# A written order for three chunks instead of two

## The chip, the cores and the metric

The kernel runs on one core of a Trainium2 chip. The metric is the device time of one execution in microseconds (us), as the median of several executions. The five engines are named as in the profile: PE (TensorE: matmuls; its weight loads are shown as PEld), DVE (VectorE), ACT (ScalarE), POOL (GpSimd) and SP (SyncE, which here only issues transfers). Each engine takes its instructions in the order in which they stand in its queue.

## The reference

Four batches of 768 positions go through a windowed attention with 8 heads of 64, and then through a gated feed-forward layer of 1024:

```python
k_sum = k.reshape(B, H, nb, block, D).max(axis=3)      # block 32
v_sum = v.reshape(B, H, nb, block, D).mean(axis=3)
scores_l = where(|i - j| < 16, q @ k.T / 8, -1e9)
scores_s = q @ k_sum.T / 8 + log(32)
a = softmax(concat([scores_l, scores_s]))
x = a @ concat([v, v_sum])                              # B, S, 512 after the heads are joined
h = relu(x @ w_in)                                      # 512 -> 1024
conv = sum over 3 taps of conv_w[k] * h[shifted by k - 1]
out = (h * sigmoid(conv)) @ w_out                       # 1024 -> 512
```

## The kernel before

**Tiles.** The work is cut into 8 chunks of 384 positions (a batch has two). A chunk has four head pairs, so there are 32 attention steps, numbered n = 0 to 31 (chunk n // 4). For each n the keys' windows (`kw`), the block maxima (`ks`), the values (`va`) and block means (`vm`, from the sums `vs` and a matmul `pv`) are prepared; `qk` makes the scores in PSUM, `mx` adds the mask and finds the maxima (DVE), `ex` takes the exponentials with their sums (ACT), `sm` and `rc` make the reciprocals, `nr` normalizes (POOL or DVE); j = 2n + h counts the halves: `tr` j transposes them on PE, `cp` j copies them out (ACT or DVE), `av` n multiplies by the values, `xh` and `xl` split the result into a high and a low part (ACT, DVE).

**The feed-forward part.** A chunk has 8 units u of 128 features. `f` c.u.cc is one quarter of unit u's first product (three matmuls: high by high, low by high, high by low). Then come, in this order, `re` (relu, ACT), `ta` (the middle tap, ACT or DVE), two `cv` (the other taps, DVE), `th` (tanh, ACT), `mu` (the gate, DVE), `gh` and `gl` (high and low part of the gated rows, ACT and POOL). `g` st.fc, called `second` in the code, is a piece of the second product for 128 rows of the output (three matmuls), `ob` copies a finished tile out and stores it. The first product has three PSUM banks: unit u + 3 needs `mu` of unit u. The transposes have one bank, the second product one.

**What sets the order.** Three regimes follow one another:

1. The table `ORDER` is a string of steps. `run` calls them one by one inside `tc.manual_schedule()`, and each engine gets its instructions in just that order. A letter at the end of a step names the engine (a: ACT, p: POOL, v: DVE). `w` 9 is nine idle matmuls on PE.
2. From chunk `FIRST` on, loops write the steps: `unit(c, u, ...)` calls `slot_t` (transposes), `slot_av`, `slot` (preparation of the steps ahead and the scores of n = j // 2), the unit's own steps, and 2 to 4 pieces of the second product. There only PE keeps the order in which the steps are written; a scheduler places the other engines' instructions by its own costs.
3. At the seam, the first `slot` of chunk `FIRST` is held behind the last instructions of the table on SP and DVE (`last`, which `run` fills from the steps that return an instruction: the transfers, and `mu`).

Where a slot's n begins a batch (chunk of even number), the slot also writes `vs`, `pv`, `vm` and `ks` of that n:

```python
            if n < npair:
                if at(n)[3] == 0:
                    vs(n)
                    pv(n)
                    v_mean(n)
                V(n)
                if at(n)[3] == 0:
                    k_max(n)
                kb(n)
```

In chunk c the first unit's slot prepares n = 4c + 6: 14 for chunk 2, 18 for chunk 3. Transfers wait on SP in the order in which they are issued. R loads a pair's keys, K its windows, T and V the values, Q the queries, I and O the weights; M spreads the means.

Of the kernel before, what the change touches and what calls it, by code (L numbers as in the profile page):

```python
# [51 lines left out]
rc1 mx2.0.1 pv1 mx2.0.2 cp1a Q5 mx2.1.0 ex2.0.2 nr1.0p mx2.1.1 ex2.0.1 mx2.1.2 qk3 ex2.1.0 sti1
V2 ex2.1.1 T10 vb0 locw tr2 hii1 ex2.1.2 I3 nr1.1v cp2a win6 mx3.0.0 V3 ex2.0.0 w3 tr3 mx3.0.1
zcw mx3.0.2 av0 wli1 sm2 ex3.0.0 mx3.1.0 mx3.1.1 ex3.1.0 rc2 O0 mx3.1.2 ex3.0.2 qk4 nr2.0v cp3a
stcw ex3.0.1 nr2.1v tr4 I2 vm1 pv2 loi5 ex3.1.2 vb1 cp4v xh0 ex3.1.1 mx4.0.0 xl0 wli0 tr5 sm3
zi5 rc3 av1 mx4.0.1 mx4.0.2 vm2 ex4.0.1 mx4.1.0 sti5 pv3 ex4.0.2 xh1 mx4.1.1 nr3.0p mx4.1.2
ex4.0.0 cp5v qk5 ex4.1.2 kb6 xl1 vb2 hii5 vs10 tr6 ex4.1.0 f0.0.0 nr3.1p cp6a av2 mx5.0.0
# [18 lines left out]
f1.0.3 wlo5 mx9.0.2 hio4 mu0.7 f1.1.2 ex8.0.0 ks10 f1.2.0 re1.0 wlo4 ex8.1.2 f1.1.3 ta1.0v
ex8.0.2 f1.2.1 mx9.1.0 vm10 cv1.0.0 ex8.1.0 M10 gl0.6 g0.4 ex9.1.0 mx9.1.1 K11 cv1.0.2 sm8 re1.1
f1.2.2 M8 kb10 rc8 mx9.1.2 th1.0 nr8.0p pv11 ta1.1v V8 g0.5 zo6 V10 cv1.1.0 nr8.1p tr16 gh0.7
K12 qk10 mu1.0 ex9.1.1 gl0.7 cv1.1.2 ex9.0.0 f1.3.0 ex9.1.2 mx10.0.0 loo6 cp16a f1.2.3 ex9.0.1
sto6 T9 f1.3.1 th1.1 K13 mx10.0.1 tr17 ex9.0.2 mu1.1 f1.3.2 zo7 loo7 f1.4.0 mx10.0.2 hio6  # L80
mx10.1.0 f1.3.3 sto7 sm9 cp17a f1.4.1 vm11 rc9 wlo6 mx10.1.1 ex10.0.0 av8 mx10.1.2 re1.2 ks11
hio7 f1.4.2 nr9.0p ex10.1.1 ta1.2v M12 g0.6 gh1.0 Q12 kb11 cv1.2.0 xh8 wlo7 tr18 ex10.0.2
cv1.2.2 qk11 gh1.1 cp18v ex10.1.0 f1.4.3 nr9.1p th1.2 g0.7 ex10.0.1 gl1.1 mu1.2 tr19 vs9 ob0
f1.5.0 kb12 re1.3 g1.0 mx11.0.0 xl8 ta1.3a f1.5.1 ex10.1.2 cv1.3.0 ex11.0.0 pv9 g1.1 mx11.0.1
sm10 gh1.2 mx11.0.2 rc10 mx11.1.0 f1.5.2 nr10.0p vm9 cv1.3.2 cp19a M9 g1.2 re1.4 mx11.1.1 V9
gl1.2 mx11.1.2 ex11.0.2 f1.5.3 M11 th1.3 Q14 tr20 nr10.1p ex11.1.1 mu1.3 qk12 ex11.1.0 ta1.4v
gl1.0 re1.5 f1.6.0 cv1.4.0 ex11.1.2 g1.3 ex11.0.1 kb13 cv1.4.2 f1.6.1 mx12.0.0 th1.4 av9 cp20a
mu1.4 ta1.5a mx12.0.1 tr21 sm11 cv1.5.0 ex12.0.1 M13 g1.4 xh9 V11 gh1.3 xl9 f1.7.0 V13 cp21a
mx12.0.2 f1.6.2 K15 ex12.0.2 mx12.1.0 cv1.5.2 V12 f1.7.1 ex12.0.0 K14 rc11 th1.5 mx12.1.1 f1.6.3
nr11.0p mx12.1.2 gh1.4 mu1.5 av10 re1.6 gl1.3 ex12.1.0 tr22 xh10 f1.7.2 nr11.1p cp22v ex12.1.2  # L90
qk13 ta1.6v gh1.5 gl1.4 tr23 mx13.0.0 g1.5 gl1.5 mx13.0.1 cv1.6.0 ex13.0.1 f1.7.3 ex12.1.1 xl10
g1.6 cp23a mx13.0.2 cv1.6.2 ex13.0.2 av11 sm12 mx13.1.0 th1.6 rc12 mx13.1.1 nr12.0p mx13.1.2
# [6 lines left out]
def attention_ffn(ctx, tc, qT, kT, vT, k_win, v_nat, v_win, w_in, cwT, w_out, mask8, ident_in, out):  # L99
# [121 lines left out]
    def keys(n):  # L221
        if n not in kw:
            if n == NP - 1:
                t = sp.tile([P, 1024], F32, tag="stage", name=f"kw{n}", bufs=2)
# [46 lines left out]
        nc.vector.tensor_reduce(ks[b, p], kv, AX.X, ALU.max)  # L271

    def win(n):
# [3 lines left out]
        (nc.gpsimd if n else nc.vector).tensor_copy(keys(n)[:, :, :WK], k)  # L277

    def kb(n):
        c, p, b, hf = at(n)  # L280
        nc.gpsimd.tensor_copy(
            keys(n)[:, :, WK:NK], ks[b, p].unsqueeze(1).to_broadcast([P, CB, NB])
        )

# [22 lines left out]
                stop=i == S // P - 1,  # L307
            )

    def v_mean(n):  # L310
# [2 lines left out]
        nc.scalar.activation(vm[b, p], pvs.pop(n)[:NB, :P], AF.Copy, scale=1.0 / BLK)

    def vb(n):
        c, p, b, hf = at(n)
        nc.gpsimd.tensor_copy(
            va[n][WK:NK, :, :], vm[b, p].unsqueeze(1).to_broadcast([NB, CB, P])
        )

# [44 lines left out]
            accum_out=sm[n][:, h, i : i + 1],  # L365
        )

    def sums(n):
        nc.scalar.activation(sm[n], sm[n], AF.Copy, bias=1e-9)

    def rc(n):
        nc.vector.reciprocal(sm[n], sm[n])
# [47 lines left out]
        for new, old in zip(xT[c], xT[c - 1]):  # L420
            nc.vector.tensor_copy(new[:, :, 0:2], old[:, :, CH - 2 : CH].bitcast(F32))  # L421
# [4 lines left out]
    def xl(n):
        h, l = rows(n)
# [21 lines left out]
        hf = c % 2  # L449
        return CH - 1 + 2 * hf, (CH - 1) * hf  # L450

    def re(c, u):
# [1 line left out]
        nc.scalar.activation(h, h, AF.Relu)  # L454
# [46 lines left out]
    def gh(c, u):
        nc.scalar.copy(gate_rows("hi", c, u), conv[c, u])  # L502

    def gl(c, u):
        nc.gpsimd.tensor_tensor(  # L505
            gate_rows("lo", c, u),
            conv.pop((c, u)),
            gate_rows("hi", c, u).bitcast(F32),
            ALU.subtract,
        )  # L510
# [257 lines left out]
```

## Time and profile before

| | us |
|---|---|
| median of 3 runs (390.04 to 390.67) | 390.18 |
| the profiled execution | 390.11 |
| its span | 388.3 |
| PE busy | 370.9 |
| ACT busy | 250.3 |
| DVE busy | 247.0 |
| POOL busy | 150.3 |

The span is the time from the first to the last recorded instruction; what lies around it is 1.8 us in that execution. Busy time is the time in which an engine has at least one instruction under way. PE's matmuls overlap, so a busy PE isn't always at its peak: the granted clock (PEclk) tells at which share of full speed it ran, in tenths in the slices. A row of a timeline gives start, duration, engine, line, operation, output and inputs, and in brackets the idle time ahead and what ended it. A row of the chain of waits gives only start, length and what the time went to. Chunk c starts with its first `f`: chunk 2 at 108.8 us, chunk 3 at 154.6 us, chunk 4 at 195.2 us.

### The profile page before, as it was taken

What the parts mean: (1) busy time and instruction counts of PE and PEld (TensorE: products, weight loads), DVE (VectorE), ACT (ScalarE), POOL (GpSimd) and SP (SyncE); (2) the same over time, 40 slices, a digit from 0 to 9 for tenths busy, and PEclk for the clock granted to TensorE, in tenths of its full rate; (3) what the DMA queues carried; (4) which work ended last, traced back from release to release, by engine and by line L of the source; (5) the groups of instructions that cost most, each with busy time, mean ns of one, the idle gap of its engine ahead of it and who ended that gap; (6) DMA issues with size and microseconds to landing.
All of it is one profiled execution on the core that took longest, in us unless ns stands there. A gap on an engine that the chain in (4) does not pass through costs nothing.

```text
span 388.3 us, 8833 instructions
## 1 busy us (share of the span) xinstructions
PE 370.9 (96%) x3164; PEld 317.8 (82%) x3167; DVE 247.0 (64%) x764; ACT 250.3 (64%) x795; POOL 150.3 (39%) x186
## 2 busy tenths in 40 slices
...
PEclk9999999999969999999989999999999999999999
...
GB/s 281 364 317 329 277 212 284 217 187 122 298 289 245 145 144 132 197 191 88 100 93 103 117 97 101 75 120 95 105 67 0 30 9 20 29 28 27 29 54 54
DMA packets 26859, 55.03 MB, mean 142 GB/s; under 512 B 3072, under 2 KB 11456, under 8 KB 26816
## 3 DMA queue, kind: packets, MB, share of 16 engines
...
q8 instruction: 25, 0.41, 0.5%
...
## 4 chain that ended last, share of the span: by engine, by line
PE 80%; ACT 8%; DVE 6%; DMA 3%; issue 1%; POOL 1%; SPq 0%; ACTq 0%; POOLq 0%; DVEq 0%
PE f L524 31%; PE f L440 30%; PE xp L398 6%; PE pt L384 6%; PE pq L330 5%; ACT a L359 3%; DVE t L474 2%; DMA kT<-kT 2%; DMA kw<-k_win 1%; PE pv L302 1%; ACT t L485 1%; DVE t L492 1%; DVE a L344 1%; ACT wu_i L145 1%; DVE ks L271 1%
## 5 line engine op out<-in xcount | busy, mean ns | idle before, releaser
L505 POOL TENSOR_TENSOR glo<-t,ghi 128x383 fp32r<-128x383 f32 (+1 forms) x64 | 64.9, 1016 | 124.1 <-ACT ghi L502 113.3
L440 PE MATMUL f<-xh,win_hi 128*128 128x384 f32 (+1 forms) x256 | 92.8, 362 | 2.9 <-DVE t L492 2.9
L440 PE MATMUL f<-xh,win_lo 128*128 128x384 f32 (+1 forms) x256 | 87.8, 343 | 0.0
L440 PE MATMUL f<-xl,win_hi 128*128 128x384 f32 (+1 forms) x256 | 87.8, 343 | 0.0
L474 DVE SCALAR_TENSOR_TENSOR t<-f,cw,t 128x382 f32<-128x382 f32 (+3 forms) x128 | 78.8, 615 | 13.6 <-ACT t L463 10.7
L359 ACT ACTIVATE a<-a,nm 128x120 f32<-128x120 f32 x192 | 73.7, 385 | 5.3 <-DVE nm L344 4.9
L524 PE MATMUL f<-wout_hi,ghi 128*128 128x512 f32 x192 | 76.4, 398 | 0.0
L524 PE MATMUL f<-wout_lo,ghi 128*128 128x512 f32 x192 | 75.7, 394 | 0.0
L524 PE MATMUL f<-wout_hi,glo 128*128 128x512 f32 x192 | 75.2, 393 | 0.0
L485 ACT ACTIVATE t<-t 128x383 f32<-128x383 f32 (+1 forms) x64 | 33.6, 525 | 45.6 <-DVE t L474 44.6
L376 POOL TENSOR_TENSOR a<-a,sm 128x360 f32<-128x360 f32 x59 | 47.7, 825 | 34.3 <-ACT f L454 16.3
L492 DVE SCALAR_TENSOR_TENSOR t<-t,f 128x383 f32<-128x383 f32 (+1 forms) x64 | 35.4, 554 | 31.2 <-ACT t L485 31.0
L440 PEld LDWEIGHTS f<-xh,win_hi 128*128 128x128 f32 x256 | 49.1, 192 | 7.3 <-DVE t L492 2.1
L440 PEld LDWEIGHTS f<-xl,win_hi 128*128 128x128 f32 x256 | 49.2, 192 | 1.5 <-DVE xl L428 0.2
L440 PEld LDWEIGHTS f<-xh,win_lo 128*128 128x128 f32 x256 | 49.1, 192 | 0.3 <-POOL win_lo L182 0.3
L344 DVE CUSTOM_DVE_ANT_0 a<-pq,mask 128x120 f32<-128x120 f32 x192 | 44.1, 275 | 2.7 <-PE pt L384 1.6
L524 PEld LDWEIGHTS f<-wout_hi,glo 128*128 128x128 f32 x192 | 36.3, 189 | 8.1
L524 PEld LDWEIGHTS f<-wout_hi,ghi 128*128 128x128 f32 x192 | 36.5, 190 | 6.3 <-ACT ob L534 0.5
L454 ACT ACTIVATE f<-f 128x384 f32<-128x384 f32 (+1 forms) x64 | 30.4, 475 | 16.3 <-PE f L440 15.7
L524 PEld LDWEIGHTS f<-wout_lo,ghi 128*128 128x128 f32 x192 | 36.4, 190 | 5.3
L465 DVE TENSOR_SCALAR t<-f,cw 128x385 f32<-128x385 f32 (+1 forms) x41 | 25.3, 617 | 23.3 <-ACT f L454 21.6
L384 PE MATMUL pt<-consts,a 128*120 128x128 f32 x192 | 33.4, 283 | 6.7 <-DVE xh L421 2.7
...
## 6 DMA issues: line engine op xcount, KB each, us to landing
...
```

Source lines behind the costliest of these rows:

```text
L344: nc.vector.tensor_tensor_reduce(aa[n, h][:, i, :], pq[n][h][:, i * NK : (i + 1) * NK], mask[:, {(0, 0): 0, (1, 2): 2}.get((hf, i), 1), :] ...
L359: nc.scalar.activation(a, a, AF.Exp, bias=nm[n][:, h, i : i + 1], scale=-1.0, accum_out=sm[n][:, h, i : i + 1],)
L376: engine[e].tensor_tensor(a, a, sm[n][:, h, :].unsqueeze(2).to_broadcast([P, 3, NK]), ALU.mult)
L384: nc.tensor.transpose(pt[j][:NK, i * P : (i + 1) * P], a[:, i, :], ident)
L440: nc.tensor.matmul(f1ps[c, u][:, :n], w[:, u, cc, :], x[:, cc, :n], start=(cc == 0 and m == 0), stop=(cc == NCC - 1 and m == 2),)
L454: nc.scalar.activation(h, h, AF.Relu)
L465: nc.vector.tensor_scalar(t, h, cw[:, u, 1:2], 1.0, ALU.mult, ALU.mult)
L474: nc.vector.scalar_tensor_tensor(t[:, i0:i1], f1ps[c, u][:, hf + k - 1 + i0 : hf + k - 1 + i1], cw[:, u, k : k + 1], t[:, i0:i1], ALU.mult ...
L485: nc.scalar.activation(t, t, AF.Tanh, scale=0.5)
L492: return nc.vector.scalar_tensor_tensor(t, t, 1.0, h, ALU.add, ALU.mult)
L505: nc.gpsimd.tensor_tensor(gate_rows("lo", c, u), conv.pop((c, u)), gate_rows("hi", c, u).bitcast(F32), ALU.subtract,)
L524: nc.tensor.matmul(f2ps[b, st], g[:, fc, ss], w[:, fc, :], start=(fc == 0 and m == 0), stop=(fc == NFC - 1 and m == 2),)
```

## The change

`FIRST` becomes 3, and the table is new: it has 1011 steps instead of 757, and ends with the last step of chunk 2's units. Of the steps that are common to both, the places differ nearly everywhere, and some go to other engines: the copies 2, 3, 6, 7, 11, 17, 19 and 20 from ACT to DVE, 4, 5 and 14 from DVE to ACT, a few taps each way, and the normalizations 3.0 and 7.1 from POOL to DVE. The idle matmuls come in two steps more evenly sized (9, 5, 4, 2, 3 become 12, 6, 5; 23 in both). The functions get an engine letter more; the new table uses none of the new letters. The copied key spans of chunk 1 (`win4` to `win7`) and the sums of batch 0 by products (`pv0` to `pv3`) are in both tables.

```diff
-FIRST = 2
+FIRST = 3
 ORDER = """
-R0 I7 Q0 R1 R2 R3 Q1 ks0 I6 win0 T0 kb0 zi7 loi7 I0 qk0 I1 sti7 hii7 ks1 win1 Q2 wli7 mx0.0.0 T1
+R0 Q0 R1 I1 R3 R2 Q1 ks0 I2 win0 T0 kb0 qk0 Q2 win1 ks1 I0 kb1 mx0.0.0 zi1 T1 loi1 mx0.0.1
...
-g1.7 mu1.6 ex13.1.2 re1.7 tr24 gh1.6 ta1.7v ex13.1.1 gl1.6 cv1.7.0 ex13.1.0 ex13.0.0 cv1.7.2
-nr12.1p sm13 ob1 rc13 nr13.1p th1.7 xh11 mu1.7 nr13.0p xl11 gh1.7 cp24v gl1.7
+ob4 f2.6.3 sm17 gh2.5 rc17 nr17.0v re2.6 nr17.1p ta2.6a cv2.6.0 gl2.5 f2.7.0 cv2.6.2 gl2.4 th2.6
+f2.7.1 mu2.6 f2.7.2 f2.7.3 re2.7 ta2.7a cv2.7.0 cv2.7.2 th2.7 gh2.6 mu2.7 gl2.6 gh2.7 gl2.7
 """
...
+    engine = {"p": nc.gpsimd, "v": nc.vector}
+    copy = {"a": nc.scalar.copy, "p": nc.gpsimd.tensor_copy, "v": nc.vector.tensor_copy}
...
-    def re(c, u):
+    def re(c, u, e="a"):
         h = f1ps[c, u][:, : CH + 2 * (c % 2)]
-        nc.scalar.activation(h, h, AF.Relu)
+        if e == "a":
+            nc.scalar.activation(h, h, AF.Relu)
+        else:
+            nc.vector.tensor_scalar(h, h, 0.0, None, ALU.max)
...
```

Three places show what the table moves. The names are those of the tiles: `f1_2_0` is the first product of chunk 2's unit 0, `f2_0_1` a tile of the second product, `pt24` the bank of transpose 24, `t2_7` the gate of chunk 2's unit 7; the number after the last underscore counts tiles.

PE where chunk 1 ends and chunk 2 begins, before:

```order
L440 MATMUL f1_1_7_1539<-xh1_765,win_lo_68 128x386
...
L524 MATMUL f2_0_1_1401<-wout_hi_69,ghi_791 128x512
L524 MATMUL f2_0_1_1401<-wout_lo_70,ghi_791 128x512
L524 MATMUL f2_0_1_1401<-wout_hi_69,glo_797 128x512
L384 MATMUL pt24_1674<-consts_65,a12_0_1500 120x128 x3
L384 MATMUL pt25_1711<-consts_65,a12_1_1553 120x128 x3
L440 MATMUL f1_2_0_1717<-xh2_1347,win_hi_67 128x384
```

And now:

```order
L467 MATMUL f1_1_7_1604<-xh1_742,win_lo_68 128x386
L467 MATMUL f1_2_0_1673<-xh2_1404,win_hi_67 128x384
L467 MATMUL f1_2_0_1673<-xl2_1405,win_hi_67 128x384
L467 MATMUL f1_2_0_1673<-xh2_1404,win_lo_68 128x384
L554 MATMUL f2_0_2_1617<-wout_hi_69,ghi_788 128x512
L554 MATMUL f2_0_2_1617<-wout_lo_70,ghi_788 128x512
L554 MATMUL f2_0_2_1617<-wout_hi_69,glo_823 128x512
L467 MATMUL f1_1_7_1604<-xh1_742,win_hi_67 128x386
```

Chunk 2's first unit was behind the two transposes; now its first quarter stands among those of chunk 1's last unit, ahead of both.

DVE around the sum `vs18`, which `pv18` on PE needs (`pv18` is PE's instruction ahead of `f1_3_0` in both kernels; before, four pieces of the second product stand ahead of it, now the last matmul of `f1_2_7`). Before:

```order
L492 SCALAR_TENSOR_TENSOR t2_2_1867<-t2_2_1867,f1_2_2_1853 128x383
L372 RECIPROCAL sm15_1925<-sm15_1925 128x6
L474 SCALAR_TENSOR_TENSOR t2_3_1966<-f1_2_3_1952,cw_66,t2_3_1966 128x382
L287 TENSOR_REDUCE vs18_2281<-vt18_2049 128x24
L474 SCALAR_TENSOR_TENSOR t2_3_1966<-f1_2_3_1952,cw_66,t2_3_1966 128x383
```

And now:

```order
L522 SCALAR_TENSOR_TENSOR t2_6_2243<-t2_6_2243,f1_2_6_2155 128x383
L504 SCALAR_TENSOR_TENSOR t2_7_2265<-f1_2_7_2247,cw_66,t2_7_2265 128x382
L504 SCALAR_TENSOR_TENSOR t2_7_2265<-f1_2_7_2247,cw_66,t2_7_2265 128x383
L522 SCALAR_TENSOR_TENSOR t2_7_2265<-t2_7_2265,f1_2_7_2247 128x383
L307 TENSOR_REDUCE vs18_2280<-vt18_1782 128x24
L291 TENSOR_REDUCE ks18_2288<-kT18_1834 128x24
```

The sum stood in the middle of chunk 2, beside unit 3; now it is behind the gate of unit 7, the table's last step on DVE.

ACT in the last units of chunk 2, before:

```order
L454 ACTIVATE f1_2_6_2140<-f1_2_6_2140 128x384
L485 ACTIVATE t2_5_2110<-t2_5_2110 128x383
L463 ACTIVATE t2_6_2154<-f1_2_6_2140,cw_66 128x383
L502 CAST ghi_791<-t2_5_2110 128x383
L485 ACTIVATE t2_6_2154<-t2_6_2154 128x383
```

And now:

```order
L515 ACTIVATE t2_5_2153<-t2_5_2153 128x383
L383 ACTIVATE a17_0_2160,sm17_2218<-a17_0_2160,nm17_2159 128x120 x2
L383 ACTIVATE a17_1_2200,sm17_2218<-a17_1_2200,nm17_2159 128x120
L532 CAST ghi_788<-t2_4_2091 128x383
...
L532 CAST ghi_788<-t2_5_2153 128x383
L482 ACTIVATE f1_2_6_2155<-f1_2_6_2155 128x384
L493 ACTIVATE t2_6_2243<-f1_2_6_2155,cw_66 128x383
L515 ACTIVATE t2_6_2243<-t2_6_2243 128x383
L482 ACTIVATE f1_2_7_2247<-f1_2_7_2247 128x384
```

The exponentials of n = 17 and the casts now stand between unit 5's tanh and unit 6's relu, and unit 7's relu is directly behind unit 6's tanh. Before, unit 6's relu was ahead of unit 5's tanh, and the exponentials behind unit 6's cast.

More of the change, by code (lines that the diff above doesn't have):

```diff
@@ L52 @@
[L52 to L57, printed above, removed]
@@ L76 @@
[L76 to L81, printed above, removed]
@@ L82 @@
[L82 to L92, printed above, removed]
-g1.7 mu1.6 ex13.1.2 re1.7 tr24 gh1.6 ta1.7v ex13.1.1 gl1.6 cv1.7.0 ex13.1.0 ex13.0.0 cv1.7.2
@@ new lines @@
+wli6 ex4.1.0 av2 M4 locw ex4.1.2 mx5.0.0 hii3 tr7 stcw mx5.0.1 vb3 f0.0.1 xh2 mx5.0.2 ex5.0.0
+f0.1.1 mx5.1.0 cp7v wli3 sm4 ex5.0.2 f0.2.1 mx5.1.1 zo0 xl2 ex5.1.0 av3 loo0 ex5.1.1 sto0 O2
+ex5.0.1 f0.0.2 Q7 rc4 xh3 loi4 f0.2.2 M5 zi4 mx5.1.2 nr4.0p xl3 f0.1.2 Q8 hio0 sti4 f0.0.3
+ex5.1.2 wli5 ks8 tr8 hii4 f0.1.3 re0.0 vs8 f0.2.3 sm5 ta0.0a kb6 nr4.1p qk6 cp8a cv0.0.0 O1 zi7
+R9 loi7 tr9 re0.1 rc5 V5 sti7 re0.2 M7 mx6.0.0 nr5.0p ta0.1a cv0.0.2 cp9a K8 mx6.0.1 wli4 th0.0
+cv0.1.0 w5 av4 ta0.2a V6 mu0.0 hii7 mx6.0.2 win7 f0.3.0 cv0.1.2 xh4 nr5.1p mx6.1.0 zo2 f0.3.1
@@ new lines @@
+cv0.2.0 th0.1 mx6.1.1 kb7 f0.3.2 ex6.0.1 loo2 tr10 ex6.0.2 mx6.1.2 wli7 O7 cv0.2.2 qk7 gh0.0 R10
+mu0.1 cp10a th0.2 sto2 f0.4.0 ex6.0.0 tr11 mx7.0.0 wlo0 ex6.1.1 mu0.2 f0.3.3 ex6.1.0 mx7.0.1
+f0.4.1 cp11v ex6.1.2 gl0.0 ex7.0.0 mx7.0.2 f0.4.2 ks9 sm6 zo1 f0.5.0 ex7.0.1 loo1 gh0.1 f0.5.1
+sto1 O3 re0.3 K9 f0.4.3 xl4 gl0.1 hio2 M6 f0.5.2 mx7.1.0 gh0.2 ta0.3v Q9 av5 kb8 ex7.1.0 mx7.1.1
+gl0.2 cv0.3.0 ex7.0.2 f0.5.3 ex7.1.1 rc6 cv0.3.2 nr6.0p re0.4 g0.0 mx7.1.2 th0.3 ta0.4v nr6.1p
+qk8 re0.5 mu0.3 hio1 loo7 f0.6.0 ta0.5a cv0.4.0 wlo1 tr12 xh5 ed4 f0.6.1 cv0.5.0 gh0.3 zo7
@@ new lines @@
+cv0.4.2 gl0.3 g0.1 cp12a xl5 O5 f0.6.2 th0.4 wlo2 mx8.0.0 V7 cv0.5.2 zo3 pv8 f0.6.3 mx8.0.1
+ex7.1.2 mu0.4 tr13 vm8 kb9 sm7 mx8.0.2 f0.7.0 ex8.0.0 sto7 re0.6 g0.2 mx8.1.0 cp13a loo3 ta0.6a
+f0.7.1 rc7 O6 sto3 th0.5 f0.7.2 cv0.6.0 nr7.0p gh0.4 av6 hio7 mx8.1.1 loo5 zo5 mx8.1.2 wlo7
+cv0.6.2 f0.7.3 ex8.1.0 O4 mu0.5 tr14 th0.6 K10 qk9 sto5 re0.7 R11 cp14a nr7.1v f1.0.0 Q10 gh0.5
+loo6 K12 tr15 xh6 mu0.6 gl0.5 f1.0.1 hio3 xl6 f1.1.0 cp15a ks10 wlo3 ta0.7a av7 zo6 cv0.7.0
+f1.1.1 ex8.1.2 gl0.4 T9 mx9.0.0 xh7 cv0.7.2 f1.0.2 Q12 ex8.0.1 xl7 f1.1.2 Q11 kb10 ex8.1.1 sto6
@@ new lines @@
+g0.3 ex8.0.2 sm8 loo4 th0.7 f1.1.3 rc8 zo4 nr8.0p mu0.7 f1.0.3 gh0.6 mx9.0.1 T10 f1.2.0 sto4
+re1.0 K11 tr16 mx9.0.2 gl0.6 hio4 f1.2.1 M8 mx9.1.0 mx9.1.1 V8 ta1.0a f1.2.2 mx9.1.2 wlo4 hio5
+cv1.0.0 qk10 cp16a cv1.0.2 hio6 f1.2.3 nr8.1p vs9 K13 th1.0 g0.4 V11 re1.1 wlo5 mu1.0 ex9.1.1
+V10 tr17 mx10.0.0 re1.2 pv9 V9 f1.3.0 ta1.1v vm9 T17 wlo6 gh0.7 g0.5 vs10 M9 ex9.1.2 f1.3.1
+gh1.0 cv1.1.0 gl0.7 ex9.0.2 pv10 g0.6 cv1.1.2 ex9.0.0 ex9.1.0 cp17v f1.3.2 kb13 th1.1 ta1.2v
+g0.7 ex9.0.1 mx10.0.1 sm9 f1.3.3 vm10 rc9 ob0 mx10.0.2 nr9.0p ks11 av8 nr9.1p re1.3 mu1.1 g1.0
@@ new lines @@
+M12 cv1.2.0 gl1.0 tr18 T11 mx10.1.0 g1.1 Q13 mx10.1.1 kb11 mx10.1.2 M10 f1.4.0 cv1.2.2 kb12 Q14
+qk11 cp18v th1.2 ex10.1.2 mu1.2 tr19 ta1.3a mx11.0.0 g1.2 mx11.0.1 xh8 mx11.0.2 f1.5.0 gh1.1
+cp19v ex10.1.0 gl1.1 f1.4.1 mx11.1.0 cv1.3.0 ex10.0.2 g1.3 gh1.2 cv1.3.2 ex10.0.0 f1.4.2 vs11
+ex10.1.1 g1.4 ex10.0.1 mx11.1.1 T19 sm10 xl8 f1.4.3 th1.3 K14 vs17 g1.5 re1.4 ex11.0.0 f1.5.1
+rc10 mu1.3 T16 nr10.0p ex11.0.2 av9 Q15 mx11.1.2 ex11.0.1 ta1.4v nr10.1p R17 ex11.1.0 g1.6 xh9
+V13 gl1.2 ex11.1.1 tr20 xl9 qk12 ex11.1.2 cp20v kb14 sm11 pv11 f1.6.0 mx12.0.0 K15 mx12.0.1
@@ new lines @@
+f1.5.2 cv1.4.0 f1.6.1 rc11 mx12.0.2 nr11.1p tr21 f1.5.3 nr11.0p cp21a mx12.1.0 mx12.1.1 g1.7
+ex12.0.0 cv1.4.2 re1.5 mx12.1.2 tr22 th1.4 f1.6.2 cp22v ex12.0.2 qk13 ob1 mu1.4 kb15 ta1.5v
+f1.6.3 vm11 cv1.5.0 f1.7.0 M11 re1.6 V12 cv1.5.2 tr23 ex12.0.1 g2.0 R16 gh1.4 vs16 M13 ex12.1.0
+gl1.4 f1.7.1 th1.5 mx13.0.0 av10 mx13.0.1 ex12.1.2 mx13.0.2 ex12.1.1 mu1.5 g2.1 gh1.3 mx13.1.0
+M14 ks17 sm12 gl1.3 ta1.6a f1.7.2 ex13.1.0 f2.0.0 mx13.1.1 R19 xh10 cv1.6.0 g2.2 V14 gh1.5 xl10
+ex13.0.0 f1.7.3 mx13.1.2 cp23a cv1.6.2 f2.0.1 ex13.0.2 rc12 nr12.0p re1.7 av11 th1.6 gl1.5
@@ new lines @@
+ex13.1.1 tr24 mu1.6 ex13.1.2 g2.3 ta1.7v ex13.0.1 nr12.1p f2.0.2 xh11 cv1.7.0 qk14 xl11 cv1.7.2
+f2.1.0 K17 cp24v th1.7 g2.4 M15 mx14.0.0 gh1.6 mu1.7 K16 sm13 pv17 gl1.6 f2.0.3 mx14.0.1 T18
+mx14.0.2 tr25 re2.0 f2.2.0 ex14.0.1 ta2.0v f2.1.1 gh1.7 mx14.1.0 g2.5 cv2.0.0 ex14.0.0 gl1.7
+cp25a mx14.1.1 f2.1.2 cv2.0.2 vm17 g2.6 rc13 th2.0 ks16 nr13.0p ex14.1.0 f2.1.3 ex14.1.1 nr13.1p
+mx14.1.2 R18 tr26 mu2.0 f2.2.1 Q16 kb16 gh2.0 pv16 qk15 re2.1 ex14.0.2 g2.7 cp26a mx15.0.0 K18
+mx15.0.1 f2.2.2 ta2.1v ob2 f2.3.0 cv2.1.0 f2.2.3 mx15.0.2 cv2.1.2 g3.0 re2.2 vm16 f2.3.1 th2.1
@@ new lines @@
+ex14.1.2 tr27 f2.3.2 sm14 mx15.1.0 mx15.1.1 g3.1 mx15.1.2 mu2.1 f2.3.3 ta2.2v gh2.1 g3.2 rc14
+cv2.2.0 nr14.0p av12 cv2.2.2 gl2.0 g3.3 xh12 nr14.1p ex15.0.1 f2.4.0 xl12 ex15.1.1 g3.4 th2.2
+cp27a qk16 mu2.2 gh2.2 f2.4.1 re2.3 K19 gl2.2 f2.5.0 ta2.3a f2.4.2 ex15.0.2 kb17 tr28 g3.5
+mx16.0.0 mx16.0.1 f2.4.3 cp28v mx16.0.2 g3.6 cv2.3.0 tr29 cv2.3.2 g3.7 mx16.1.0 mx16.1.1 f2.5.1
+mx16.1.2 ob3 av13 ex15.0.0 g4.0 ex16.1.0 M17 cp29v ex15.1.2 f2.5.2 V15 ed12 re2.4 Q17 g4.1 xh13
+Q18 ex15.1.0 xl13 f2.5.3 M16 ta2.4a g4.2 V16 sm15 th2.3 rc15 V17 cv2.4.0 nr15.1p av14 ex16.0.0
```

86 lines of the change are left out of this document (42 added, 44 removed).

## The prediction

> **What bounds the kernel now.** I read the page first (busy shares, the slices), then busy time by stretches, then every idle time of TensorE (PE) with what ended it, then the chain of waits around the two longest. The page:
>
> ```profile
> PE 370.9 (96%) x3164; PEld 317.8 (82%) x3167; DVE 247.0 (64%) x764; ACT 250.3 (64%) x795; POOL 150.3 (39%) x186
> PEclk9999999999969999999989999999999999999999
> ```
>
> PE is busy for 96% of the span, and the edit changes neither the number nor the shape of its matmuls (23 idle ones in both tables). What can change is the time in which PE waits, and the time after a wait in which its clock is halved: the two slices marked 6 and 8. By stretches (columns: stretch, length, busy us of PE, weight loads, DVE, ACT, POOL, granted clock, DMA share, GB/s):
>
> ```profile
> 0.00:40.00 40.00, 35.45 (x406) 24.26 (x410) 31.39 (x123) 31.82 (x117) 23.52 (x34) 1.00 0.98 321
> 40.00:80.00 40.00, 36.99 (x363) 31.85 (x363) 39.43 (x121) 36.90 (x115) 27.95 (x29) 1.00 0.78 248
> 80.00:100.00 20.00, 19.95 (x225) 16.77 (x222) 15.25 (x52) 16.77 (x59) 11.93 (x17) 1.00 0.52 158
> 108.00:116.00 8.00, 7.70 (x29) 6.95 (x31) 5.42 (x9) 1.53 (x3) 1.41 (x3) 0.62 0.94 295
> ```
>
> From 40 to 80 us DVE is the bound (39.43 of 40); from 80 on it is PE, until the stretch at half clock. PE's idle times there, and the later one like it:
>
> ```profile
> 105.01 0.54 PE L384 MATMUL pt<-consts,a 128*120 128x128 f32 x3 [1.51 <-POOL a L376]
> 108.30 0.87 PE L384 MATMUL pt<-consts,a 128*120 128x128 f32 x3 [2.74 <-DVE xh L421]
> 194.93 0.51 PE L384 MATMUL pt<-consts,a 128*120 128x128 f32 x3 [1.94 <-ACT aT L389]
> ```
>
> The first two are the end of the written table: tr24 and tr25 wait for the last copies and products of chunk 1, and nothing of chunk 2 stands ahead of them on PE. The chain of waits shows what the half clock adds (start, us, what):
>
> ```profile
> 108.30 0.87 PE pt L384 x3
> 109.17 3.84 PE f L440 x12
> 113.00 2.65 PE f L524 x9
> 117.61 0.47 PE pt L384 x3
> 118.08 2.09 PE f L440 x12
> 120.18 2.08 PE f L524 x9
> ...
> 151.99 2.77 PE f L524 x12
> 154.87 2.12 PE f L440 x12
> 195.44 3.28 PE f L440 x12
> 198.72 3.18 PE f L524 x12
> ```
>
> Twelve matmuls of the first product took 3.84 instead of 2.09, nine of the second 2.65 instead of 2.08, the transpose 0.87 instead of 0.47: 1.75 + 0.57 + 0.40 = 2.7 us. With 1.51 + 2.74 = 4.25 idle, the seam from chunk 1 to 2 costs 6.95 us. At 195 us, half clock adds (3.28 - 2.12) + (3.18 - 2.77) = 1.6.
>
> **The change, part by part.** *The old seam.* The new table has f2.0 between the pieces of f1.7, and goes on with chunk 2's products: when tr24 and tr25 come, PE has other work on both sides. I take the whole 6.95 off; at worst only the half clock and the 2.74 go (5.4), since tr24 still waits for POOL's product.
>
> *The new seam.* PE's row after the last matmul of f2.7 is pv18, the transpose of vs18. vs18 is now behind mu2.7 on DVE, and the first unit of chunk 3 is behind pv18. mu2.7 needs f2.7 itself. So PE must wait for a chain, and cannot take f3.0, which is ready. The durations come from the same steps in chunk 2 and before it:
>
> ```profile
> 152.76 0.47 ACT L454 ACTIVATE f<-f 128x384 f32<-128x384 f32 x1
> 153.32 0.58 ACT L463 ACTIVATE t<-f,cw 128x383 f32<-128x383 f32 x1
> 145.56 0.58 ACT L463 ACTIVATE t<-f,cw 128x383 f32<-128x383 f32 x1
> 146.17 1.27 DVE L474 SCALAR_TENSOR_TENSOR t<-f,cw,t 128x382 f32<-128x382 f32 x2
> 147.47 0.53 ACT L485 ACTIVATE t<-t 128x383 f32<-128x383 f32 x1 [0.67 <-DVE t L474]
> 147.90 0.46 ACT L389 COPY aT<-pt 120x384 f32<-120x384 f32 x1
> 148.03 0.55 DVE L492 SCALAR_TENSOR_TENSOR t<-t,f 128x383 f32<-128x383 f32 x1 [0.59 <-ACT t L485]
> 142.67 0.95 DVE L287 TENSOR_REDUCE vs<-vt 128x24 f32<-128x768 f32 x1 [0.42 <-PE pv L297]
> ```
>
> From start to start: relu to tap 0.56 (152.76 to 153.32); tap to the two convolution steps 0.61 (145.56 to 146.17); these to tanh 1.30 (147.47); tanh to the next on ACT 0.43 (147.90); tanh to mu 0.56 (148.03). ACT's order in the new table is re2.6, ta2.6, th2.6, re2.7, ta2.7, th2.7, so unit 7's relu is behind unit 6's tanh. From re2.6: 0.56 + 0.61 + 1.30 + 0.43 = 2.90 to re2.7, then 0.56 + 0.61 + 1.30 + 0.56 = 3.03 to mu2.7, 0.48 to vs18 (DVE's step after a mu started 0.48 later), 0.95 for vs18: pv18 stands 7.4 after re2.6.
>
> When does re2.6 start? Put f2.6.1 at 0 on PE. Its seven groups to the end of f2.7 take 7 x 2.09 / 4 = 3.66. ACT's tanh of unit 5 is behind xh15, which needs av15; PE ended that a transpose and a second-product group earlier (0.33 and 0.69), so th2.5 stands at about -0.6. Then ACT has six exponentials, two gh, ob4 and sm17 before re2.6:
>
> ```profile
> 184.23 2.38 ACT a L359 x12
> 142.97 0.59 ACT L534 ACTIVATE ob<-f 128x512 f32<-128x512 f32 x1
> 143.44 0.25 ACT L313 ACTIVATE vm<-pv 24x128 f32<-24x128 f32 x1
> 96.61 0.50 ACT L502 CAST ghi<-t 128x385 fp32r<-128x385 f32 x1
> 97.02 0.47 ACT L454 ACTIVATE f<-f 128x386 f32<-128x386 f32 x1
> ```
>
> That is th2.5 0.43, six exponentials 2.38, two gh 0.82 (0.41 from 96.61 to 97.02), ob4 0.47 (142.97 to 143.44), sm17 0.1: 4.2, so re2.6 at 3.6 and pv18 at 11.0. PE is idle from 3.66 to 11.0: **7.4 us**. At the least (ACT waits for nothing but f2.6) re2.6 is at 1.6 and the idle time 5.35; at the most, with one more late tanh of the kind seen later, about 9. After it comes half clock, 1.6 to 2.7 by the two cases above; I take 2.15. pv18 and tr33 themselves stand in both kernels.
>
> [...]
>
> *The head.* The new table starts with other weights, and gives DVE more copies and products. Counted ahead of the mu1.2 that frees f1.5's bank, DVE has three more aT copies, two more normalizations, two taps fewer:
>
> ```profile
> L389 DVE COPY aT<-pt 120x384 f32<-120x384 f32 x6 | 3.3, 555 | 1.0 <-PE pt L384 0.8
> L376 DVE TENSOR_TENSOR a<-a,sm 128x360 f32<-128x360 f32 x5 | 2.6, 525 | 0.0
> L465 DVE TENSOR_SCALAR t<-f,cw 128x385 f32<-128x385 f32 (+1 forms) x41 | 25.3, 617 | 23.3 <-ACT f L454 21.6 <-POOL glo L505 1.7
> 5.20 0.95 DVE L271 TENSOR_REDUCE ks<-kT 128x24 f32<-128x768 f32 x1 [4.07 <-DMA kT<-kT]
> ```
>
> 3 x 0.555 + 2 x 0.525 - 2 x 0.617 = 1.5 us more on the engine that bounds the stretch, while PE at f1.5 is 0.5 further (three groups of f fewer at 0.52, three second-product groups more at 0.69). That is up to 1.0 lost; PE had slack to hide some of it, and I take 0.5. The gain is bounded by DVE's idle time of the first 40 us: 40 - 31.39 - 5.2 before the first kT = 3.4.
>
> *Transfers and the rest.*
>
> ```profile
> 171.84 4.84 DMA kw<-k_win
> 177.14 0.95 DVE L271 TENSOR_REDUCE ks<-kT 128x24 f32<-128x768 f32 x1 [0.83 <-POOL kw L281]
> ```
>
> R16 to R19, K16 to K19 and T16 to T19 move into the table, on SP's queue, ahead of V14 to V17. Loads run two to four steps ahead of their use and the DMA share was 0.52 from 80 to 100 us, so I cost them at nothing; if that cover is gone, one late k_win transfer is the price, 4.84 us, of which PE sees what its queue doesn't cover. POOL loses and gains nothing on PE's path but kb18, which follows ks18 and is needed 6 us after pv18. Chunk 3's maxima for batch 3 stay where they were on DVE, each behind POOL's copy and that behind a k_win transfer (the second row). They end in the idle 1.94 at 195 us. Nothing in that order is changed, so I leave its 1.94 + 1.6 = 3.54 in.
>
> **The sum**: -6.95 + 7.4 + 2.15 + 0.5 = +3.1. Against the profiled execution, 388.3 of span in 390.11, that gives 393.2; the median, 390.18, is 0.07 above that execution. **Forecast 393.2 us**, slower by 0.8%. A difference under 0.2% (0.78 us: 389.4 to 391.0) can't be told from none.
>
> **Rivals.**
> - *The new wait at its floor.* ACT is early, re2.6 follows f2.6 at once: 5.35 idle, 1.6 of half clock; with the head, -6.95 + 5.35 + 1.6 + 0.5 = +0.5: 390.6, the same. For it: ACT is only 84% busy from 80 to 100. Against: xh15 ties ACT to PE four steps earlier.
> - *The stall at 195 us goes.* Chunk 3 begins with PE late, so DVE has caught up, and the k_win transfers meet less traffic: -3.54, 389.6; on the edge of faster. Against: same rows, same waits.
> - *The head gains* (the other side). The first queries and keys are now loaded ahead of weights; if DVE's idle 3.4 us all go and the 0.5 isn't lost, 393.2 - 3.9 = 389.3. It decides only from 3.8 us on. Against: DVE's list is longer.
> - *Chunk 3 trips.* POOL's copy for n = 21 now stands ahead of the normalizations of n = 18, and waits for a transfer that waits for qk18. If that lands late, tr36 waits: 3 us more, 396.
>
> **How the numbers follow.** Forecast's case (idle 6.5 to 9, 391.5 to 395) 0.58; floor 0.13; stall gone 0.11 (half faster, half same); head 0.10; trip 0.08. Faster 0.16, same 0.18, slower 0.66. The range 389.2 to 396.3 leaves out the lower part of the stall and head cases and the end of the trip, under 2 in 10; the likeliest case's own range is 391.5 to 395.
>
> **What would show it.** Right: no idle time of PE over 2 us and clock 1.0 from 97 to 140 us; one idle time of 5 to 9 us before a pv matmul (the transpose of vs18) at about 148 to 156, released by DVE vs; a half-clock stretch behind it; the stall at the end of chunk 3 still there. Wrong: pv18 finds vs18 done, or PE comes to f2.7 late, because DVE or ACT held it all through chunk 2; or chunk 1's first unit starts over 3 us earlier than here:
>
> ```profile
> 62.47 0.45 PE L440 MATMUL f<-xh,win_hi 128*128 128x386 f32 x1
> ```

## The result, and the profile after

The changed kernel takes 394.62 us (median of 4 runs, 393.85 to 394.99), against 390.11 for the kernel before on the same chip: a ratio of 1.0116, 95% interval 1.0089 to 1.0143. The profiled execution took 394.99 with a span of 393.2; the forecast was 393.2 us, the range 389.2 to 396.3. The page of the changed kernel:

```profile
PE 371.7 (95%) x3167; PEld 316.6 (81%) x3167; DVE 255.1 (65%) x776; ACT 246.4 (63%) x786; POOL 148.4 (38%) x183
PE   8899889999999992999989999999999999999996
PEclk9999999999999997699999999999999999999999
```

The weak slices around 107 and 195 us are gone from PEclk; a new pair, marked 7 and 6, stands around 155 us, and PE is nearly empty in the first of them (the 2). The waits of PE, longest first (what waited for what, us in total, times, longest):

```profile
PE pv L317 <- DVE vs L307: 7.7, 1, 7.7
PE pt L411 <- ACT aT L416: 3.5, 4, 1.8
PE xp L425 <- DVE xl L455: 1.9, 2, 1.5
```

The longest is the one forecast: pv18 waits for vs18:

```profile
157.46 0.37 PE L317 MATMUL pv<-consts,vs 128*24 128x128 f32 x1 [7.71 <-DVE vs L307]
```

The chain of waits through it, from ACT's first late step on (start, us, what):

```profile
147.40 1.15 ACT a L383 x6
148.55 0.49 ACT ob L564
...
149.65 0.40 ACT ghi L532
150.05 0.39 ACT f L482
...
152.44 0.52 ACT t L515
152.96 0.39 ACT f L482
...
155.34 0.53 ACT t L515
...
155.90 0.55 DVE t L522
156.45 0.87 DVE vs L307
...
157.46 0.37 PE pv L317
157.83 0.64 PE pt L411 x3
158.47 3.86 PE f L467 x12
162.33 2.65 PE f L554 x9
```

Exponentials, the output copy and a cast stand ahead of re2.6 (150.05); then follow tanh 6 (152.44), re2.7 (152.96), tanh 7 (155.34), mu2.7 (155.90), vs18 (156.45), pv18 (157.46). Behind it twelve matmuls of f3.0 take 3.86 at a granted clock of 0.50, where they take 2.12 at full clock (154.87 us in the kernel before).

To see where the rest went, I took at each unit's first matmul its start, less the PE work that stands ahead of it in the written order, each matmul at its price at full clock, from start to start in these traces (0.175 us one of the first product, 0.23 one of the second, 0.42 a transpose, 0.78 a `qk`, 0.85 an `av`, 0.216 an idle one). This lag grows only where PE waits or runs slower than these prices; its changes from one unit to the next are the reading. In us:

| at | before | after | between this and the line above |
|---|---|---|---|
| f1.0 | 11.4 | 14.5 | head: +3.1 |
| f1.7 | 14.1 | 15.5 | chunk 1: -1.7 |
| f2.1 | 21.5 | 15.8 | old seam: 7.4 against 0.3, -7.1 |
| f2.7 | 21.4 | 17.0 | chunk 2: +1.2 |
| f3.1 | 21.5 | 27.4 | new seam: +10.4 |
| f3.6 | 21.6 | 28.4 | chunk 3: +0.8 |
| f4.1 | 25.2 | 30.0 | stall at the end of chunk 3: 3.5 against 1.6, -1.9 |
| f7.7 | 25.4 | 30.2 | nothing |

The last column adds up to +4.8, the difference of the spans (393.2 - 388.3 = 4.9), to rounding.

The 1.2 of chunk 2 are no waits: from f2.1 to f2.7 PE is never idle in the changed kernel. There PE goes from an attention step (a transpose, `qk`, `av`, `pv`) to a feed-forward matmul 15 times, in the kernel before 4 times. Behind such a step the first matmul takes about 0.26 us (first product) or 0.32 (second) to the next start in these traces, instead of 0.175 and 0.23. Eleven more of these are about 1 us. No run varies this alone.

### The profile page after: what moved, and what is told of

It is laid out like the page before. It is cut to its first block, busy times and chain, and to the rows that moved or that the text cites. A ratio compares the mean times of both kernels' runs of the same rounds, so it can differ in the third digit from the quotient of the medians.

```text
span 393.2 us, 8828 instructions
## 1 busy us (share of the span) xinstructions
PE 371.7 (95%) x3167; PEld 316.6 (81%) x3167; DVE 255.1 (65%) x776; ACT 246.4 (63%) x786; POOL 148.4 (38%) x183
## 4 chain that ended last, share of the span: by engine, by line
PE 74%; DVE 11%; DMA 7%; ACT 3%; issue 2%; SPq 1%; POOL 0%; ACTq 0%; DVEq 0%; POOLq 0%
PE f L554 32%; PE f L467 29%; PE xp L425 5%; PE pt L411 5%; PE pq L354 4%; DVE t L504 3%; DMA raw_b<-w_in 2%; DMA raw_a<-w_in 2%; DMA kw<-k_win 1%; DVE a L368 1%; ACT a L383 1%; DVE t L522 1%; DMA mask<-mask 1%; DVE ks L291 1%; ACT t L515 1%
## 5 line engine op out<-in xcount | busy, mean ns | idle before, releaser
L554 PE MATMUL f<-wout_hi,ghi 128*128 128x512 f32 x192 | 77.2, 402 | 0.0
L403 POOL TENSOR_TENSOR a<-a,sm 128x360 f32<-128x360 f32 x56 | 44.5, 810 | 52.8 <-DVE sm L399 35.4
L532 ACT CAST ghi<-t 128x383 fp32r<-128x383 f32 (+1 forms) x64 | 32.5, 508 | 10.3 <-DVE t L522 10.3
```

The lines of the kernel that those rows point to most:

```text
L403: engine[e].tensor_tensor(a, a, sm[n][:, h, :].unsqueeze(2).to_broadcast([P, 3, NK]), ALU.mult)
L532: copy[e](gate_rows("hi", c, u), conv[c, u])
L554: nc.tensor.matmul(f2ps[b, st], g[:, fc, ss], w[:, fc, :], start=(fc == 0 and m == 0), stop=(fc == NFC - 1 and m == 2),)
```

## The experiments

Experiments 1 to 4 ran on one chip, 5 to 8 on another. Each ratio is to the kernel before on the same chip, with its 95% interval (medians there: 389.8 us of 19 runs, 387.64 to 394.36; 389.18 of 13 runs, 387.97 to 391.75). The changed kernel was not run again beside them, so a difference from its 394.62 is one across chips. Single times of one kernel lay up to 1.2% around their median, so places in the traces carry the readings, by the lag above; the medians stand beside them. A trace is one execution, and not always one near the median. Each kernel is the changed one with the edit shown, unless it says otherwise. Where a step moves into the table, the slot leaves it out.

**1. vs18 alone.**

```diff
-... ex17.0.2 xl15 ex17.0.1 mu2.5 ex17.1.0 ...
+... ex17.0.2 xl15 ex17.0.1 mu2.5 vs18 ex17.1.0 ...
```

> The changed kernel with one more step in the table: vs18 stands behind mu2.5 on DVE, and the first slot of chunk 3 leaves it out; everything else is written as it was. Theory (the 7.71 us before pv18 are the wait for vs18, which stands behind mu2.7): the wait before pv18 goes; PE runs on through f3.0 and is held next by qk18, since ks18 is still behind mu2.7, for about 2.7 us. Time 394.6 - 10.4 + 2.7 = 387, or up to 389.6 if the shorter wait halves the clock too. Rival (PE would be held at the seam anyway, by the transposes' bank and the copies on ACT behind th2.7): the wait moves to tr34 and keeps most of its length, 392 to 395.

391.1 us (10 runs, 389.25 to 392.43), ratio 1.0024, interval 0.9992 to 1.0056; profiled 389.6. The median lies above the theory's 387 to 389.6 and below the rival's 392 to 395. The wait before pv18 is gone; PE is held next by qk18, as the theory had it, and the half clock comes behind that wait (0.50 from 160.92 to 164.33 us):

```profile
159.65 0.84 PE L354 MATMUL pq<-kw,q 64*64 64x120 f32 x24 [3.81 <-POOL kw L301]
157.18 0.55 DVE L522 SCALAR_TENSOR_TENSOR t<-t,f 128x383 f32<-128x383 f32 x1
157.65 0.95 DVE L291 TENSOR_REDUCE ks<-kT 128x24 f32<-128x768 f32 x1
157.31 2.03 POOL L535 TENSOR_TENSOR glo<-t,ghi 128x383 fp32r<-128x383 f32 x2 [3.99 <-DVE xl L455]
159.29 0.30 POOL L301 COPY kw<-ks 128x144 f32<-128x144 f32 x1
```

3.81 instead of 2.7: ks18 is behind mu2.7, which came 1.3 us later than in the changed kernel (157.18 against 155.90), since taps of f3.0, which PE now did early, stand ahead of it on DVE; and POOL's kb18 stands behind two other products. The lag from f2.7 to f3.2 is 5.3 us instead of 10.5. So one reduction's place on DVE cost some 5 us in the profiled executions, and 3.5 by the medians of the two chips. The rival, a wait at the transposes, did not come.

**2. The last lines of the table in another order.**

```diff
-... ex17.1.0 f2.6.2 gh2.4 ex17.1.2 ex17.1.1 ex17.0.0 ob4 f2.6.3 sm17 gh2.5 ... re2.6 ... th2.6 f2.7.1 mu2.6 ... re2.7 ta2.7a
+... ex17.1.0 f2.6.2 ex17.1.2 ex17.1.1 f2.6.3 re2.6 ta2.6a ex17.0.0 ... sm17 ... gh2.4 ... re2.7 th2.6 mu2.6 ta2.7a ... ob4 gh2.5
```

> The changed kernel with only the last lines of the table in another order: re2.6 and ta2.6 stand ahead of the last exponential of n = 17, re2.7 ahead of th2.6, ob4 and gh2.5 behind ta2.7. vs18 stays behind mu2.7. Theory (the length of the wait is the chain re2.6 to mu2.7, which starts late because ACT has the exponentials, ob4 and two gh ahead of re2.6): mu2.7 comes 2.9 us earlier, the wait is 4.8 instead of 7.7, the half clock stays: 391.7. Rival (the length is set by something that ACT's order does not move, such as the landing of T18): 394.6.

395.32 us (4 runs, 392.79 to 397.03), ratio 1.0166, interval 1.0096 to 1.0236; profiled 392.79. The wait before pv18 is 6.73, not 4.8: re2.6 came 1.8 us earlier, and one step later the gain was mostly lost:

```profile
156.97 0.37 PE L317 MATMUL pv<-consts,vs 128*24 128x128 f32 x1 [6.73 <-DVE vs L307]
148.19 0.47 ACT L482 ACTIVATE f<-f 128x384 f32<-128x384 f32 x1
152.93 0.58 ACT L493 ACTIVATE t<-f,cw 128x383 f32<-128x383 f32 x1 [1.74 <-POOL glo L535]
151.91 0.99 POOL L535 TENSOR_TENSOR glo<-t,ghi 128x383 fp32r<-128x383 f32 x1
```

The gate tile `t` has three buffers. Unit 7's tap needs unit 4's, which gl2.4 frees; with gh2.4 behind sm17, gl2.4 (151.91) came behind a normalization on POOL, and ta2.7 waited 1.74 for it. The wait follows ACT's order, against the rival, but the edit opened a second tie, so it shows only part of the theory. At f4.1 the lag is 2.1 us less than in the changed kernel: 1.0 of it is the shorter wait, and the rest, by my estimate, mostly the half clock, which would have cost about 1.6 here instead of 2.7; the mean clock of this execution was 0.991, of the changed kernel's 0.986. The median shows no gain; the profiled execution was the fastest of the four.

**3. The wait filled with idle matmuls.**

```diff
+        pi = ps.tile([P, 512], F32, tag="x", name="pi", bufs=1)
+        for _ in range(30):
+            nc.tensor.matmul(pi, idle[:, :P], idle, start=True, stop=True)
```

(behind the table's last step)

> The changed kernel with 30 idle matmuls (0.216 us each, 6.5 us) on PE between the last matmul of f2.7 and pv18. Nothing waits less: pv18 still comes when vs18 is done. Theory (the slow matmuls behind the wait are the half clock that the wait causes, 2.7 us): granted clock 1.0 behind pv18, 394.6 - 2.7 = 391.9. Rival (they are slow for another reason, transfers or cold operands): 394.6.

394.55 us (4 runs, 391.67 to 397.24), ratio 1.013, interval 1.0049 to 1.0212; profiled 391.67. The median did not move (the theory had 391.9, which only the profiled execution reached), so the times settle nothing; the trace does. By stretches, of the changed kernel first and then of this one (busy us of PE, weight loads, DVE, ACT, POOL, clock, DMA share, GB/s):

```profile
150.00:158.00 8.00, 0.54 (x3) 0.54 (x4) 5.56 (x9) 4.06 (x10) 4.60 (x5) 0.70 0.08 29
158.00:170.00 12.00, 12.00 (x93) 10.91 (x92) 7.71 (x22) 4.70 (x16) 1.88 (x4) 0.77 0.85 264
```

```profile
150.00:158.00 8.00, 6.78 (x34) 3.04 (x32) 5.53 (x10) 4.19 (x9) 4.34 (x5) 1.00 0.09 34
158.00:170.00 12.00, 12.00 (x106) 10.71 (x105) 9.40 (x26) 6.54 (x23) 2.27 (x5) 1.00 0.82 261
```

```profile
157.73 0.27 PE L317 MATMUL pv<-consts,vs 128*24 128x128 f32 x1 [1.23 <-DVE vs L307]
```

pv18 comes no earlier (157.73), the clock is 1.00 throughout, and from 158 to 170 us 106 matmuls are done instead of 93 with nearly the same DMA share. The lag from f2.7 to f3.1 is 7.7 instead of 10.4 (the filling not counted as work): in these two executions the half clock costs 2.7 us, and neither transfers nor cold operands do.

**4. The seam written into the table.** vs18 as in 1; the last lines as in 2; pv18 and tr33 ahead of f2.7.0, vm18 and cp33 ahead of gh2.4, ks18 behind mu2.7, kb18 behind gl2.6.

> vs18 behind mu2.5, pv18 and tr33 ahead of f2.7's first quarter, their copies vm18 and cp33 ahead of gh2.4, ks18 and kb18 directly behind mu2.7 and gl2.6, and the table's last lines in the order of the other experiment. Theory: no idle time over 1 us at the seam, clock 1.0 there; 394.6 - 7.7 - 2.7 = 384.2, which is 6 us under the kernel before. Rival (chunk 3's first steps are short of something that the wait had hidden, since DVE and ACT caught up in it): a new wait in units 0 to 2 of chunk 3, 387 to 390.

388.67 us (10 runs, 386.86 to 389.84), ratio 0.9979, interval 0.9945 to 1.0012: 6 us better than the changed kernel, 4.5 short of the theory, and a time in the rival's range. The trace names the places, none over 2 us:

```profile
154.41 0.50 PE L554 MATMUL f<-wout_hi,ghi 128*128 128x512 f32 x1 [1.26 <-ACT ob L564]
153.29 0.58 ACT L493 ACTIVATE t<-f,cw 128x383 f32<-128x383 f32 x1 [0.98 <-POOL glo L535]
193.35 0.52 PE L411 MATMUL pt<-consts,a 128*120 128x128 f32 x3 [1.89 <-ACT aT L416]
```

The first follows from ob4's late place behind the tap, which waited for gl2.4 as in 2: that is a wait of the kind the rival names, but one that the edit made. The last row is the old stall at the end of chunk 3, which now had its half clock again (0.50 from 194.68 to 198.09 us; 1.6); that one was in the forecast's sum as a wait without it.

**5. The stall at the end of chunk 3, in the kernel before.** The chain of waits there, in the kernel before, read forward: nr20 on POOL, kb23, then ks27 on DVE, which writes the buffer that kb23 reads, and only behind it the outer taps (`cv`) of units 5 and 6, whose tanh stands ahead of the copy that PE waits for:

```profile
188.20 0.79 POOL a L376
188.99 0.26 POOL kw L281
...
189.27 0.95 DVE ks L271
190.22 0.54 DVE t L474
```

What starts behind this wait, at 195.2 us, is f3.7, the last unit of chunk 3; chunk 4's first `f` comes at 201.7 us.

```diff
+                    with contextlib.ExitStack() as late:
+                        if n >= 26:
+                            late.enter_context(tc.issue_after(gate[3, 7]))
-                    k_max(n)
+                        k_max(n)
```

(`gate` holds the instruction of each `mu`; the lines that fill it are left out here. The edit is called `hold` below.)

> The kernel before; only the maxima ks26 and ks27 of batch 3 are held behind mu3.7 on DVE. Theory (the stall at the end of chunk 3 is ks27, which stands in DVE's queue ahead of the taps of unit 6 and waits for POOL's copy kb23 out of the same buffer): the 1.94 us of idle time at 195 us and the half clock behind it (1.6) go, 390.1 - 3.5 = 386.6, or 388.2 where no half clock followed. Rival (the transposes there wait for the copies on ACT and the k_win transfers whatever DVE does): no change, 390.1.

387.1 us (10 runs, 385.62 to 389.04) against 389.18, ratio 0.9942, interval 0.9911 to 0.9973. The stretch, before and in this kernel:

```profile
190.00:205.00 15.00, 13.06 (x101) 11.54 (x100) 8.81 (x28) 8.04 (x26) 4.62 (x6) 0.89 0.27 80
```

```profile
190.00:205.00 15.00, 15.00 (x119) 12.98 (x119) 10.41 (x30) 9.00 (x27) 4.82 (x6) 1.00 0.31 98
```

Of PE's waits in this kernel, by the timeline, two stand ahead of that stretch:

```profile
94.43 0.96 PE L398 MATMUL xp<-aT,va 120*64 120x64 f32 x24 [1.92 <-DMA va<-v_win]
111.70 0.52 PE L384 MATMUL pt<-consts,a 128*120 128x128 f32 x3 [4.44 <-DVE aT L389]
```

The stall and its half clock are gone: the lag from f3.5 to f4.1 is 0.0 instead of 3.6, which is the theory's 3.5. The median fell by 2.1, between the theory's 3.5 and the 1.9 that it had where no half clock followed. The profiled execution, one of the slower ones, also shows a late v_win transfer at 94 us that the profile of the kernel before has not. Whether the other runs had it too can't be read from their times.

**6. The changed kernel with both repaired.** As 4 with `hold` as in 5, and these last lines:

```diff
+... mu2.5 vs18 ex17.1.0 f2.6.2 gh2.4 gl2.4 ex17.1.2 f2.6.3 re2.6 ta2.6a ex17.1.1 ex17.0.0 cv2.6.0 cv2.6.2
+sm17 f2.7.0 pv18 tr33 rc17 nr17.0v nr17.1p vm18 cp33 f2.7.1 f2.7.2 f2.7.3 th2.6 mu2.6 re2.7 ta2.7a cv2.7.0
+cv2.7.2 ob4 gh2.5 gl2.5 th2.7 gh2.6 mu2.7 ks18 gl2.6 kb18 gh2.7 gl2.7
```

> The changed kernel with vs18 early, pv18 and tr33 and their copies in the table, ks26 and ks27 held, and a last stretch of the table in which gh2.4 and gl2.4 stay ahead of re2.6 (they free the third buffer of the gate), and ob4 stands directly behind ta2.7. Theory (in the former order of this kind the tap of unit 7 waited for gl2.4, and the second product for ob4): no idle time over 1 us from 100 us on, clock 1.0: the former kernel's 388.5 - 1.26 - 1.89 - 1.65 = 383.7, of which up to 0.8 may stay as a smaller wait at tr35. Rival (a wait of the same length appears at the next place, qk18 behind kb18): 386 to 388.

383.46 us (4 runs, 382.85 to 385.01), ratio 0.984, interval 0.9794 to 0.9887. From 100 us on PE has no wait over 0.04 us up to its last matmul, which ends at 377.5 us, and the clock is full:

```profile
100.00:380.00 280.00, 277.44 (x2226) 242.48 (x2215) 164.30 (x487) 164.76 (x515) 87.87 (x109) 1.00 0.32 98
```

Its lag is 17.7 at f2.7, 18.0 at f3.2 and 17.9 at f4.1. What is left over the kernel before is the head and the 1.2 of chunk 2; what is won is both seams and the stall.

**7. The engines of the head put back.** As 6, with cp2, 3, 6, 7, 11, 17, 19, 20 to ACT, cp4, 5, 14 to DVE, nr3.0 and nr7.1 to POOL.

> As the kernel just named, with the engines of the first two chunks as they were before: the copies 2, 3, 6, 7, 11, 17, 19 and 20 on ACT, 4, 5 and 14 on DVE, the normalizations 3.0 and 7.1 on POOL. Theory (the new head loses 3.1 us by f1.0 and 1.4 by f1.7 because DVE, the bound from 40 to 80 us, has more to do): 2.2 us less work on DVE ahead of f1.0, which takes 1 to 2 us off the lag there and 1 off the time: 382.7. Rival (the order of the loads and weights sets the head): the same as the kernel just named, or up to 1 slower since ACT gets the copies.

383.58 us (4 runs, 382.91 to 385.01), ratio 0.984, interval 0.9786 to 0.9894: no gain. The lag at f1.0 is 15.7 against 15.0, at f1.7 17.6 against 16.2. The loss comes early:

```profile
27.34 0.54 PE L412 MATMUL pt<-consts,a 128*120 128x128 f32 x3 [1.73 <-DVE aT L417]
35.85 0.92 PE L426 MATMUL xp<-aT,va 120*64 120x64 f32 x24 [1.46 <-DVE xl L456]
```

Copies taken off DVE in one place came back on it in another (4, 5), where a transpose now waits. So my account of the head, so many more copies on DVE, does not hold as a price. The result is what the rival forecast, but the order of the loads and weights was not varied.

**8. The old table with the same repair.** The kernel before, `FIRST` = 2 as it was, `hold` as in 5, and its own last lines:

```diff
-g1.7 mu1.6 ex13.1.2 re1.7 tr24 gh1.6 ... rc13 nr13.1p th1.7 xh11 mu1.7 nr13.0p xl11 gh1.7 cp24v gl1.7
+g1.7 f2.0.0 f2.0.1 f2.0.2 mu1.6 ex13.1.2 re1.7 tr24 f2.1.0 f2.1.1 f2.1.2 gh1.6 ... rc13 nr13.1p cp24a th1.7
+xh11 mu1.7 nr13.0p xl11 tr25 f2.0.3 gh1.7 gl1.7
```

> The kernel before with its own table for chunks 0 and 1 and the loops from chunk 2 on; at the table's end f2.0 and three quarters of f2.1 stand around tr24 and tr25, cp24 goes to ACT, and ks26 and ks27 are held. Theory (all that the longer table can win is the seam from chunk 1 to 2, 6.95 us, and that needs a few matmuls of chunk 2 ahead of the two transposes, no written chunk): 390.1 - 6.95 - 3.5 = 379.7. Rival (the seam's wait moves on to unit 0 of chunk 2, where the slots' work is late since DVE and ACT do not come earlier): 383 to 386.

380.5 us (4 runs, 379.38 to 381.72), ratio 0.9759, interval 0.9712 to 0.9806; profiled 379.72. Seven quarters of chunk 2 around two transposes, and one copy on another engine, take all of the old seam away (the parts of the edit were not tried apart); the same stretch before and in this kernel:

```profile
97.00:115.00 18.00, 13.75 (x115) 11.54 (x111) 12.56 (x33) 10.35 (x35) 9.64 (x14) 0.81 0.99 294
```

```profile
97.00:115.00 18.00, 18.00 (x196) 15.30 (x196) 13.69 (x47) 13.93 (x47) 9.82 (x14) 1.00 0.99 301
```

The lag is 14.7 at f1.7, 14.9 at f2.1, 14.8 at f4.1 and 15.0 at the end: chunk 2 by the loops loses nothing, where the written chunk 2 lost 1.2. This beats both kernels, and 6 as well.

## Why the prediction was right

The time, 394.62, lies in the likeliest case's own range (391.5 to 395), 1.4 above its figure. The signs named for it came: clock 1.00 from 97 to 140 us without a wait, one idle time of 7.71 before pv18 released by vs18, half clock behind it, and the stall at the end of chunk 3. By the steps:

- *The old seam, -6.95.* Right: -7.1. Experiment 8 takes the same away from the kernel before without a written chunk 2.
- *The new seam, 7.4 idle.* Right: 7.71. From re2.6 to pv18 the prediction had 7.4; the timeline has 149.96 to 157.46, 7.5. The floor (5.35) was not reached, since ACT's six exponentials, ob4 and two casts did stand ahead of re2.6. The 0.3 more arises there: behind ob4 ACT issues the store of that tile and stands idle for 0.42, which the prediction left out. Experiment 1 shows the cause, 2 in part the length.
- *The half clock, 2.15.* It came with the wait, and the size was too small: 2.7, by the filled wait of experiment 3. That is the upper of the two cases that the prediction had, as at the old seam; behind the waits of experiments 1 (3.81) and 2 (6.73) the half clock cost about 1.6, an estimate from the lag. So the price is not one of the wait's length alone. PE was busy for 5.99 us of the half clock here and for 5.80 at the old seam, and it cost 2.7 both times; for 3.41 at 195 us in the kernel before, and it cost 1.6. What sets its length was not shown.
- *The head, 0.5.* Mis-sized: 3.1 at f1.0 (f1.0 starts at 66.28 instead of 62.47), of which chunk 1 returns 1.7, so 1.4. The reason given, DVE's longer list, is at most part of it: the next wait on that side is `av5` for xl4 on DVE (1.49 at 53 us), but experiment 7 takes steps off DVE and gains nothing. What sets the head stays open.
- *Chunk 2, nothing.* Missing term: the written chunk 2 loses 1.2 without a wait, which the loops do not; by the estimate above about 1 of it is the price of PE's changes from attention to feed-forward steps.
- *Transfers, nothing.* Nearly right. The rival that trips in chunk 3 came true at a quarter of its price: POOL's copy for n = 21 waits 3.13 for a k_win transfer, ks25 on DVE waits for that copy, and tr37 on PE waits 0.82. (Of the moved loads, R18, T18 and K16 to K19 stand behind V14, not ahead of it.)

```profile
172.51 0.31 POOL L301 COPY kw<-ks 128x144 f32<-128x144 f32 x1 [3.13 <-DMA kw<-k_win]
172.85 0.95 DVE L291 TENSOR_REDUCE ks<-kT 128x24 f32<-128x768 f32 x1 [1.59 <-POOL kw L301]
177.99 0.51 PE L411 MATMUL pt<-consts,a 128*120 128x128 f32 x3 [0.82 <-ACT aT L416]
201.36 0.52 PE L411 MATMUL pt<-consts,a 128*120 128x128 f32 x3 [1.76 <-ACT aT L416]
```

- *The stall at 195 us, left in.* Half right: the wait stays (1.76 for 1.94, the last row), its half clock does not (the clock was 1.00 from 197.58 to 204.40 us), so 1.9 of the 3.54 went. The step that failed is taking the half clock for sure behind a wait of this length; the last section has waits with it and without it.

Put together: too small by 0.3 at the idle time, 0.55 at the half clock, 0.9 at the head, 1.2 in chunk 2 and 0.8 in chunk 3, too large by 1.9 at the stall and 0.15 at the old seam. The errors went both ways, so the sum is better than its parts; that it lies so near is in part luck.
